# Recurrent outer-product attention and an MLP on one core: odd heads without a second load of v, and 48 weight columns for the state's products

## The chip, the cores and the metric

One core of one Trainium2 chip runs the whole program. The metric is the device time of one execution in microseconds (us). Three runs of the kernel before gave 453.13, 453.8 and 453.02 us, median 453.13. Engine names as in the profile: PE is TensorE (PEld its weight loads), DVE is VectorE, ACT is ScalarE, POOL is GpSimd, SP is SyncE, which here only issues DMAs.

## What is computed

```python
# q, k, v, f_logit: (B=4, H=8, S=768, D=48), float32
f = 1.0 / (1.0 + np.exp(-f_logit))
for t in range(S):
    state = f[:, :, t, :, None] * state + np.einsum('bhd,bhe->bhde', k[:, :, t], v[:, :, t])
    y[:, :, t] = np.einsum('bhd,bhde->bhe', q[:, :, t], state)
x = y.transpose(0, 2, 1, 3).reshape(B, S, 384)
xn = (x - mean(x)) / np.sqrt(var(x) + 1e-06) * g_ln
out = x + np.maximum(xn @ w_ch1, 0.0) @ w_ch2        # 384 -> 1536 -> 384
```

Each head carries a 48 x 48 state that decays by a gate per row; the heads' outputs of one time step are joined to a row of 384, and a two-layer MLP with a residual follows.

## The kernel before

**Tiling.** The sequence is cut into 12 units of 64 time steps; a unit has all 4 batches and 8 heads. In a tile of raw input, 128 partitions are two batches of 64 steps (index `b`, 0 or 1, is the half), and `g` (0 or 1) counts the two such pairs of batches. Heads go in pairs: `a` (0 to 3) is the pair, `r` (0 or 1) the head in it, and `e` (0 to 7) runs over `g` and `a`. Transposed tiles have the pair's two heads on partitions 0 to 47 and 64 to 111 (`head_rows(r)`), and 16 segments `2e + b` of 64 steps along the free axis. `half(i)` is partitions 64i to 64i+63.

**Attention of a unit n**, as a table of stages that `attention(n)` returns:
- `gates`, `after`, `upto` (L686, L701, L705): sigmoid of the transposed gate logits on ACT (L691 from unit 5 on), then two scans on DVE (L664, L676) that give products of gates from each step to the unit's end and from its start.
- `k`, `q` (L709, L722): keys times `after` give kh (L718), queries times `upto` give qh (L727).
- `kept` (L731): state times the unit's whole product, on DVE.
- `carried` (L739, matmul L748): qh times `kept` into the PSUM tile py, 32 matmuls of 48 x 64 weights and 48 columns.
- `scores` (L753, matmul L762): kh times qh into the PSUM tile ps, 32 matmuls; `causal` (L765): DVE masks them into sc.
- `values` (L785, matmul L791): sc times v is added to py, 32 matmuls; then ACT copies py to x (L798), one copy for each g.
- `chunk` (L813, matmul L821): kt times v into the PSUM tile pn, 32 matmuls with 64 weight columns, of which 48 are a head's; `state` (L825): DVE adds pn to `kept` (L829).
- `stats`, `norm`, `turn`: mean and variance on DVE, reciprocal root on POOL, the normalized rows, and their transpose on PE with the gain put on by ACT (L856).

kt is kh transposed. From unit 5 on (`DIRECT`) transposes of f, q, k and kh are not made on PE but by DMA: ACT splits a tile into two planes of 16 bits (`split`, L439), POOL sends them to DRAM (L443: fhalves, khalves, qhalves, Khalves), and SP brings them back with a DMA transpose (`transposed`, L458: `turned` for f and for q in one and the same tile, a tile for k, and kt). The transpose of f can only be issued when DVE has read the same tile as q (L727).

**Where odd heads' v comes from.** Matmul positions are (row half, column half). In `scores`, head r of batch half b puts its 64 x 64 result on PSUM rows `half(b ^ r)`, so for odd heads the two batches are exchanged. `values` therefore needs odd heads' v with the batches exchanged as well, and `load(n, "x")` (L469) fetches them a second time into the tile vx: 4 DMAs a unit, 64 partitions of four runs of 192 bytes each, 48 KB. All of v comes with `load(n, "v")` (L479), 4 DMAs of 96 KB.

**MLP of a unit** (`mlp(n)`): the first layer is L968 in units 0 to 2 and block products (`by_blocks`, L906, with ACT copies L911 and DVE additions L914) from unit 3 on; the second layer is L978 in units 0 and 1 and seven half-size products (L997) after. The output is written by SP (L985, L1010). Weights come as 64-bit floats in 12 pieces through DMAs of 768 KB (L540), and are made 32-bit by ACT, DVE and POOL (L552 to L568) in the first 80 us.

**Order.** Nothing is scheduled by a program: `START` (units 0 to 2 of the MLP) and `UNIT` (one unit of the MLP from 3 on) are plans written by hand, and every engine and every DMA queue takes its instructions in the order in which the tokens stand there. `a5.chunk` is a stage, `m4` a step of the MLP, `l6v` a load, `p6k0` a split, `x6f` a DMA transpose. In `UNIT`, `l{p}x` stands ahead of `p{p}k0`, `l{p}q` and the transpose of f, `x{p}f`.

**PSUM.** Eight banks: four single ones for the MLP and the transposes, two for py, and two with the tag "two" that ps and pn use in turn.

Of the kernel before, what the change touches and what calls it, by code (L numbers as in the profile page):

```python
# [8 lines left out]
FP32 = mybir.dt.float32  # L9
# [294 lines left out]


START = """
l0k a0.gates l0q f d d a0.after l0x d r l0v a0.kx
a0.upto f a0.kept l1f a0.k l1k d a0.q f a0.carried a0.scores a0.causal
a0.values l1q w d r d a0.stats l1x f a0.kt a1.gates w
a0.norm d a1.after l1v a0.chunk a0.turn f r a0.state a1.upto m0 d  # L310
a1.kept w a1.kx f a1.k m0 a1.q f r a1.kt r w
a1.carried d a1.scores a1.causal f l2k f l2v f w m0 a1.values
l2f r r a1.stats a1.chunk w m0 a1.norm m0 a1.turn r m0
m1 r w m1 r w l2x w f l2q w m1
f m1 a1.state a2.gates a2.after r m1 a2.kx m0 m0 r w
a2.k l3k w a2.upto a2.kept m1 a2.q m0 m0 m0 a2.carried l3q
m0 a2.scores l3v l3x a2.causal U m1 a2.values a2.stats l3f a2.norm m1
m1 m1 a3.gates m1 a2.kt m1 a2.turn a2.chunk a3.kx m2 l4f a3.after
U a3.k a3.upto U T m2 a2.state m2 a3.q a3.kept m2 a3.carried
a3.scores a3.kt U U l4v l4k a4.gates a3.causal U U U t  # L320
U a3.values a3.chunk l4q T l5v a4.after m2 l5f U a3.stats m2
a4.kx U l5k a3.norm s2 m2 p5f0 a3.state m2 a4.k U m2
p5f1 m2 a4.kt a3.turn u l6f x5f p5k0 a4.upto a4.q l4x p5k1
y3 l5q a5.gates l5x m2 m2 a4.kept m2
"""
UNIT = """
m{m} a{o}.after a{n}.kt m{m} a{n}.carried p{o}q0 a{n}.scores m{m} p{o}q1 a{n}.causal m{m} m{m}
l{p}k m{m} m{m} a{o}.upto a{n}.values x{o}q x{o}k m{m} a{n}.stats p{p}f0 p{p}f1 m{m}
m{m} a{n}.chunk m{m} a{n}.norm m{m} m{m} m{m} m{m} s{m} m{m} l{p}x p{p}k0
p{p}k1 l{p}q m{m} a{o}.q m{m} x{p}f a{n}.turn a{o}.k l{p}v p{o}K0 a{p}.gates m{m}  # L330
a{n}.state l{z}f a{o}.kept m{m} y{n} m{m} m{m} p{o}K1
"""
# [3 lines left out]
def kernel(  # L336
# [19 lines left out]
    nc = tc.nc  # L356
    B, H, S, D = q.shape
    P = 128
    T = 64
    G = B // 2  # L360
    NP = H // 2
    GA = G * NP
# [25 lines left out]
    raws = fast.enter_context(tc.tile_pool(name="raws", bufs=2))  # L388
# [8 lines left out]
    def two_banks(name, tag="two"):  # L397
        return ps2.tile([P, 2, 512], FP32, tag=tag, name=name)
# [8 lines left out]
    for name, fill in (("f", 40.0), ("q", 0.0), ("k", 0.0)):  # L407
        t = consts.tile([P, G, H, 64], FP32, name=f"{name}raw")
        nc.gpsimd.memset(t[:, :, :, D:64], fill)
        wide_heads[name] = t  # L410
    loaded = {}
# [8 lines left out]
    def raw_of(n, name):  # L420

        return wide_heads["k" if n >= DIRECT and name == "q" else name]
# [38 lines left out]
    def load(n, name, engines=(nc.sync,)):  # L461
        if n >= NU:
            return
        if name == "x":

            loaded[n, name] = raws.tile([P, G, NP, D], FP32, tag="rawx", name=f"vx{n}")
            odd = v.rearrange("b (a r) s d -> b r s a d", r=2)
            for b in range(B):
                nc.sync.dma_start(out=loaded[n, name][(1 - b % 2) * T:(2 - b % 2) * T, b // 2],  # L469
                                  in_=odd[b, 1, n * T:(n + 1) * T])  # L470
            return
        if name == "v":
            vt = raws.tile([P, G, H, D], FP32, tag="rawv", name=f"v{n}")
            loaded[n, name] = vt
        else:
            loaded[n, name] = raw_of(n, name)
        src = {"f": f_logit, "k": k, "q": q, "v": v}[name]
        for b in range(B):
            engines[b % len(engines)].dma_start(  # L479
                out=loaded[n, name][(b % 2) * T:(b % 2 + 1) * T, b // 2, :, 0:D],  # L480
                in_=src[b, :, n * T:(n + 1) * T, :].rearrange("h p d -> p h d"))

    load(0, "f", (nc.sync, nc.scalar))

    power = consts.tile([P, 2], FP32)
# [22 lines left out]
    least = consts.tile([P, NS], FP32)  # L508
    nc.vector.memset(least, 1.0)
    state = consts.tile([P, 2, GA, D], FP32)  # L510

# [122 lines left out]
    def half(i):  # L634
        return slice(64 * i, 64 * i + 64)

    def head_rows(par):
        return slice(64 * par, 64 * par + D)

    def attention(n):  # L640
# [5 lines left out]
        at = {}  # L646
# [92 lines left out]
        def do_carried():  # L739

            at["py"] = py = two_banks(f"py{n}", "out")
            if not n:
                return
            qh, kept = at["qh"], at["kept"]
            for e in range(GA):
                for b in range(2):
                    for r in range(2):
                        nc.tensor.matmul(py[half(b), r, e * D:(e + 1) * D],  # L748
                                         lhsT=qh[head_rows(r), 2 * e + b],
                                         rhs=kept[head_rows(r), b, e], start=e == 0, stop=False,  # L750
                                         skip_group_check=True)

        def do_scores():  # L753


            at["ps"] = ps = two_banks(f"ps{n}").rearrange("s r (e t) -> s r e t", t=T)
            kh, qh = at["kh"], at["qh"]
            for e in range(GA):
                for b in range(2):
                    for r in range(2):  # L760
                        seg = 2 * e + b
                        nc.tensor.matmul(ps[half(b ^ r), r, e], lhsT=kh[head_rows(r), seg],  # L762
                                         rhs=qh[head_rows(r), seg], start=True, stop=True)

        def do_causal():  # L765
# [17 lines left out]
                nc.scalar.copy(out=kt[:, g * NP:(g + 1) * NP], in_=pt)  # L783

        def do_values():  # L785
            py, sc, vt, vx = at["py"], at["sc"], loaded[n, "v"], loaded[n, "x"]
            for e, (g, a) in enumerate(pairs):
                for b in range(2):
                    for r in range(2):
                        rows = half(b ^ r)  # L790
                        nc.tensor.matmul(py[half(b), r, e * D:(e + 1) * D], lhsT=sc[rows, r, e],  # L791
                                         rhs=vx[rows, g, a] if r else vt[rows, g, 2 * a],
                                         start=n == 0 and e == 0, stop=True,
                                         skip_group_check=True)
            x_of[n] = x = xs.tile([P, G, DM], FP32, tag="x", name=f"x{n}")
            pyv = py[:, :, 0:GA * D].rearrange("t r (g a d) -> t g r a d", g=G, d=D)
            for g in range(G):
                nc.scalar.copy(out=x[:, g].rearrange("t (a r d) -> t r a d", r=2, d=D),  # L798
                               in_=pyv[:, g])

        def do_stats():
            x = x_of[n]
# [10 lines left out]
        def do_chunk():  # L813

            if n < NU - 1:
                at["pn"] = pn = two_banks(f"pn{n}")
                kt, vt = at["kt"], loaded[n, "v"]
                for e, (g, a) in enumerate(pairs):
                    for r in range(2):
                        for b in range(2):  # L820
                            nc.tensor.matmul(pn[half(r), b, e * D:(e + 1) * D],  # L821
                                             lhsT=kt[half(b), e, half(r)],
                                             rhs=vt[half(b), g, 2 * a + r], start=True, stop=True)

        def do_state():  # L825
            if n < NU - 1:
# [5 lines left out]

        return {"gates": do_gates, "after": do_after, "upto": do_upto, "kx": do_k_across,
                "k": do_k, "q": do_q, "kept": do_kept, "carried": do_carried,
                "scores": do_scores, "causal": do_causal, "kt": do_kt, "values": do_values,
                "stats": do_stats, "chunk": do_chunk, "state": do_state,
                "norm": lambda: normalize(n), "turn": lambda: turn(n)}

# [290 lines left out]
```

## Time and profile before

| | |
|---|---|
| runs | 453.13, 453.8, 453.02 us |
| profiled execution: span | 453.4 us (the page gives no time for it beside the span) |
| PE busy | 430.9 us, 95% of the span |
| PEld busy | 398.2 us, 88% |
| DVE busy | 330.3 us, 73% |
| ACT busy | 194.4 us, 43% |
| POOL busy | 145.6 us, 32% |
| mean granted TensorE clock | 0.985 |
| packets of SP's DMA queue | 182368, 49.70 MB, 58.5% of 16 engines' span |
| x copies, L798 on ACT | 24, 128x384, 475 ns each |
| issues of vx, L469 on SP | 48, median 614 ns each, 2.5 us from issue to landing |

The span runs from the first to the last instruction of one profiled execution. A line of a view names the source line, the engine, the operation, the tiles (written <- read) and a shape; of a matmul the shape is weights rows*columns and then the moving data. One float32 matmul leaves two records on PE, so 32 matmuls are "x64". "idle before" is what the engine waited, with what released it. The letters after SP and POOL in "SPq" mean the engine's queue, where DMAs are issued one after another.

### The profile page before, as it was taken

The numbers are of one execution on the slowest core, as the hardware profiler recorded it, in microseconds if no ns is written. First come the engines' busy times: TensorE is split into PE (matmuls) and PEld (weight loads), VectorE is DVE, ScalarE is ACT, GpSimd is POOL, SyncE is SP. The second block draws the span as 40 slices with busy tenths as digits, with TensorE's granted clock in tenths as the row PEclk, the third lists the DMA queues.
The fourth block names the chain that finished last, engine by engine and source line by source line (L and its number), as shares of the span: only waits on it lengthen the run. The fifth ranks groups of instructions, "written<-read, shape, count | busy, mean of one in ns | idle before, by whom it ended". The sixth has DMA issues, their size and how long they took to land.

```text
span 453.4 us, 12917 instructions
## 1 busy us (share of the span) xinstructions
PE 430.9 (95%) x5427; PEld 398.2 (88%) x5427; DVE 330.3 (73%) x528; ACT 194.4 (43%) x333; POOL 145.6 (32%) x165
## 2 busy tenths in 40 slices
PE   5689999999999999989999999999999999999993
PEld 4568886667899999989999989989999999999993
DVE  6698867553778988867888878878878778665451
ACT  2275753003234546445556356445455443241320
POOL 2213543249714124223323323324224204011020
PEclk9799999999999999989999999999999999999998
DMA  8999988251736779895889999898997781500001
GB/s 140 193 179 255 234 183 163 49 107 41 130 69 136 187 132 214 197 215 132 208 157 208 181 225 176 198 164 196 204 180 195 177 145 44 97 2 19 19 9 34
DMA packets 188690, 65.68 MB, mean 145 GB/s; under 512 B 175568, under 2 KB 181200, under 8 KB 188624
## 3 DMA queue, kind: packets, MB, share of 16 engines
q1 hardware_dynamic: 182368, 49.70, 58.5%
q0 software_dynamic: 4480, 14.68, 9.2%
q8 instruction: 44, 0.72, 0.7%
q10 hardware_dynamic: 1776, 0.40, 0.5%
q14 instruction: 22, 0.18, 0.2%
HBM read 30.67 MB, written 19.40 MB: 110 GB/s over the span
## 4 chain that ended last, share of the span: by engine, by line
PE 69%; DMA 11%; issue 6%; SPq 5%; POOL 4%; DVE 3%; ACT 1%; POOLq 0%; DVEq 0%; ACTq 0%
PE pp L997 24%; PE ph L968 9%; PE bx L906 8%; PE po L978 6%; PE by L906 6%; DMA kt<-Khalves 5%; SPq L479 3%; DMA w_0words<-in_moe_w_ch_dram 3%; PE pn L821 2%; PE py L748 2%; PE tr L656 2%; PE bz L906 2%; PE ps L762 2%; SPq L1010 2%; PE xp L854 2%
## 5 line engine op out<-in xcount | busy, mean ns | idle before, releaser
L917 ACT ACTIVATE h<-h 128x512 f32<-128x512 f32 x45 | 28.1, 630 | 54.4 <-DVE h L914 50.4
L968 PE MATMUL ph<-xt,w 128*128 128x256 f32 x216 | 48.6, 381 | 0.6 <-ACT xt L856 0.6
L968 PEld LDWEIGHTS ph<-xt,w 128*128 128x128 f32 x216 | 40.3, 190 | 6.3 <-issue 0.8
L997 PE MATMUL pp<-mixed,h 128*128 128x192 f32 x240 | 42.4, 326 | 0.0
L997 PE MATMUL pp<-mixed,s 128*128 128x192 f32 x240 | 42.0, 326 | 0.0
L997 PE MATMUL pp<-w,h 128*128 128x192 f32 x240 | 40.7, 326 | 0.0
L997 PEld LDWEIGHTS pp<-mixed,h 128*128 128x128 f32 x240 | 39.5, 190 | 0.3 <-ACT xt L856 0.3
L997 PEld LDWEIGHTS pp<-mixed,s 128*128 128x128 f32 x240 | 39.1, 190 | 0.0
L997 PEld LDWEIGHTS pp<-w,h 128*128 128x128 f32 x240 | 38.8, 190 | 0.0
L914 DVE TENSOR_TENSOR h<-h,bx 128x512 f32<-128x512 f32 x27 | 18.6, 687 | 24.8 <-PE bx L906 24.8
L1005 POOL TENSOR_TENSOR p1x<-p,x 128x192 f32<-128x192 f32 x10 | 13.1, 1311 | 71.6 <-ACT p L1012 71.6
L978 PE MATMUL po<-w,h 128*128 128x384 f32 x96 | 32.7, 490 | 0.7 <-POOL w L568 0.7
L664 DVE TENSOR_TENSOR_SCAN after<-gates,ends 128x1040 f32<-128x1040 f32 (+1 forms) x13 | 29.6, 2278 | 5.0 <-ACT gates L696 3.0
L676 DVE TENSOR_TENSOR_SCAN upto<-gates,starts 128x1040 f32<-128x1040 f32 (+1 forms) x13 | 30.1, 2314 | 0.5
L856 ACT ACTIVATE xt<-xp,gain 128x128 f32<-128x128 f32 x72 | 20.0, 376 | 23.3 <-PE xp L854 23.3
L906 PE MATMUL bx<-y,v 128*128 128x128 f32 x216 | 29.4, 279 | 0.0
L914 DVE TENSOR_TENSOR h<-h,by 128x512 f32<-128x512 f32 x36 | 24.6, 682 | 5.2 <-PE by L906 5.0
L978 PEld LDWEIGHTS po<-w,h 128*128 128x128 f32 x96 | 17.6, 190 | 12.1 <-POOL w L568 1.3
L809 POOL TENSOR_SCALAR rstd<-mv 128x2 f32<-128x2 f32 x12 | 2.8, 235 | 78.1 <-DVE mv L808 78.1
L906 PEld LDWEIGHTS bx<-y,v 128*128 128x128 f32 x216 | 26.2, 192 | 0.5
L568 POOL TENSOR_TENSOR w<-w_0upper,w_0units 128x768 int32<-128x768 int32 x7 | 12.7, 1814 | 32.8 <-DVE w_0upper L566 27.6
L997 PE MATMUL pp<-w,s 128*128 128x192 f32 x120 | 21.1, 326 | 0.0
(163 smaller groups left out, 971.7 us busy)
## 6 DMA issues: line engine op xcount, KB each, us to landing
w_0words<-in_moe_w_ch_dram SPq DMA_DIRECT2D x7, 768.0 KB, 7.2
kraw<-in_k_dram SPq DMA_DIRECT2D x48, 96.0 KB, 3.6
v<-in_v_dram SPq DMA_DIRECT2D x48, 96.0 KB, 3.8
fraw<-in_f_logit_dram SPq DMA_DIRECT2D x46, 96.0 KB, 3.6
fhalves<-fplanes POOLq DMA_DIRECT2D x14, 256.0 KB, 4.8
khalves<-kplanes POOLq DMA_DIRECT2D x14, 256.0 KB, 3.8
qhalves<-qplanes POOLq DMA_DIRECT2D x14, 256.0 KB, 3.4
Khalves<-Kplanes POOLq DMA_DIRECT2D x14, 256.0 KB, 3.7
```

What stands on the lines that cost most here:

```text
L479: engines[b % len(engines)].dma_start(out=loaded[n, name][(b % 2) * T:(b % 2 + 1) * T, b // 2, :, 0:D], in_=src[b, :, n * T:(n + 1) * T, : ...
L568: nc.gpsimd.tensor_tensor(out=to.bitcast(I32), in0=upper, in1=units, op=ALU.add)
L664: nc.vector.tensor_tensor_scan(out=at["after"].rearrange(flat)[:, c0:c1][:, ::-1], data0=gt[:, c0 + 1:c1 + 1][:, ::-1], data1=ends.rearran ...
L676: nc.vector.tensor_tensor_scan(out=at["upto"].rearrange(flat)[:, c0:c1], data0=gt[:, c0:c1], data1=starts.rearrange(flat)[:, c0:c1], initi ...
L856: nc.scalar.mul(out=xt[:, m, g * P:(g + 1) * P], in_=pt[:, m], mul=gain[:, m:m + 1])
L906: nc.tensor.matmul(banks[bank][:, i], lhsT=right[:, i * P:(i + 1) * P], rhs=left, start=new and i == 0, stop=True, skip_group_check=True)
L914: nc.vector.tensor_tensor(out=out[to], in0=out[to], in1=bank, op=op)
L917: nc.scalar.activation(out=out[to], in_=out[to] if bank is None else bank, func=AF.Relu)
L968: nc.tensor.matmul(ph[:, j], lhsT=w1[:, m, (i + j) * P:(i + j + 1) * P], rhs=xt[:, m], start=m == 0, stop=m == KD - 1)
L978: nc.tensor.matmul(po, lhsT=h[:, i, g * P:(g + 1) * P], rhs=w2[:, i], start=i == 0, stop=i == KF - 1)
L997: nc.tensor.matmul(pp, lhsT=a[:, i], rhs=b[:, i], start=i == 0, stop=i == KH - 1)
L1005: engine.tensor_tensor(out=to, in0=x1, in1=x2, op=op)
```

## The change

Three things, and what follows from them:

1. `load(n, "x")` and all its tokens are gone: 48 DMAs on SP's queue. Both heads of a pair read v from the one tile vt.
2. `scores` now leaves head r on PSUM rows `half(b)`; `values` takes its weights and v from partitions `half(b)`, and writes to `half(b ^ r)`; so does `carried`. So in py the odd heads have the batches exchanged, and the copy to x puts them right: one ACT copy of 128 partitions for the even heads, and two of 64 partitions for the odd heads, which read one half and write the other.
3. `chunk` loads 48 weight columns (`head_rows(r)`), not 64 (`half(r)`), and writes 48 PSUM rows. As `state` still reads all 128 rows, ps and pn are now one tile `shared`, allocated once, so that the 16 rows not written have numbers from the scores in them. They are used by no product.

```diff
-        if name == "x":
-            loaded[n, name] = raws.tile([P, G, NP, D], FP32, tag="rawx", name=f"vx{n}")
-            odd = v.rearrange("b (a r) s d -> b r s a d", r=2)
-            for b in range(B):
-                nc.sync.dma_start(out=loaded[n, name][(1 - b % 2) * T:(2 - b % 2) * T, b // 2],
-                                  in_=odd[b, 1, n * T:(n + 1) * T])
-            return
...
+    shared = two_banks("shared")
...
-                        nc.tensor.matmul(py[half(b), r, e * D:(e + 1) * D],
+                        nc.tensor.matmul(py[half(b ^ r), r, e * D:(e + 1) * D],
...
-            at["ps"] = ps = two_banks(f"ps{n}").rearrange("s r (e t) -> s r e t", t=T)
+            at["ps"] = ps = shared.rearrange("s r (e t) -> s r e t", t=T)
...
-                        nc.tensor.matmul(ps[half(b ^ r), r, e], lhsT=kh[head_rows(r), seg],
+                        nc.tensor.matmul(ps[half(b), r, e], lhsT=kh[head_rows(r), seg],
...
-                        rows = half(b ^ r)
-                        nc.tensor.matmul(py[half(b), r, e * D:(e + 1) * D], lhsT=sc[rows, r, e],
-                                         rhs=vx[rows, g, a] if r else vt[rows, g, 2 * a],
+                        nc.tensor.matmul(py[half(b ^ r), r, e * D:(e + 1) * D],
+                                         lhsT=sc[half(b), r, e], rhs=vt[half(b), g, 2 * a + r],
...
-            for g in range(G):
-                nc.scalar.copy(out=x[:, g].rearrange("t (a r d) -> t r a d", r=2, d=D),
-                               in_=pyv[:, g])
+            nc.scalar.copy(out=xv[:, 0], in_=pyv[:, 0])
+            for b in range(2):
+                nc.scalar.copy(out=xv[half(b), 1], in_=pyv[half(1 - b), 1])
...
-                at["pn"] = pn = two_banks(f"pn{n}")
+                at["pn"] = pn = shared
...
-                            nc.tensor.matmul(pn[half(r), b, e * D:(e + 1) * D],
-                                             lhsT=kt[half(b), e, half(r)],
+                            nc.tensor.matmul(pn[head_rows(r), b, e * D:(e + 1) * D],
+                                             lhsT=kt[half(b), e, head_rows(r)],
```

In the plans only the tokens `l0x` to `l5x` and `l{p}x` are taken out; the order of the rest stays.

More of the change, by code (lines that the diff above doesn't have):

```diff
@@ L306 @@
 START = """
-l0k a0.gates l0q f d d a0.after l0x d r l0v a0.kx
+l0k a0.gates l0q f d d a0.after d r l0v a0.kx
 a0.upto f a0.kept l1f a0.k l1k d a0.q f a0.carried a0.scores a0.causal
-a0.values l1q w d r d a0.stats l1x f a0.kt a1.gates w
+a0.values l1q w d r d a0.stats f a0.kt a1.gates w
 a0.norm d a1.after l1v a0.chunk a0.turn f r a0.state a1.upto m0 d
@@ L313 @@
 l2f r r a1.stats a1.chunk w m0 a1.norm m0 a1.turn r m0
-m1 r w m1 r w l2x w f l2q w m1
+m1 r w m1 r w w f l2q w m1
 f m1 a1.state a2.gates a2.after r m1 a2.kx m0 m0 r w
 a2.k l3k w a2.upto a2.kept m1 a2.q m0 m0 m0 a2.carried l3q
-m0 a2.scores l3v l3x a2.causal U m1 a2.values a2.stats l3f a2.norm m1
+m0 a2.scores l3v a2.causal U m1 a2.values a2.stats l3f a2.norm m1
 m1 m1 a3.gates m1 a2.kt m1 a2.turn a2.chunk a3.kx m2 l4f a3.after
@@ L322 @@
 a4.kx U l5k a3.norm s2 m2 p5f0 a3.state m2 a4.k U m2
-p5f1 m2 a4.kt a3.turn u l6f x5f p5k0 a4.upto a4.q l4x p5k1
-y3 l5q a5.gates l5x m2 m2 a4.kept m2
+p5f1 m2 a4.kt a3.turn u l6f x5f p5k0 a4.upto a4.q p5k1
+y3 l5q a5.gates m2 m2 a4.kept m2
 """
@@ L328 @@
 l{p}k m{m} m{m} a{o}.upto a{n}.values x{o}q x{o}k m{m} a{n}.stats p{p}f0 p{p}f1 m{m}
-m{m} a{n}.chunk m{m} a{n}.norm m{m} m{m} m{m} m{m} s{m} m{m} l{p}x p{p}k0
+m{m} a{n}.chunk m{m} a{n}.norm m{m} m{m} m{m} m{m} s{m} m{m} p{p}k0
 p{p}k1 l{p}q m{m} a{o}.q m{m} x{p}f a{n}.turn a{o}.k l{p}v p{o}K0 a{p}.gates m{m}
@@ L785, in do_values @@
         def do_values():
-            py, sc, vt, vx = at["py"], at["sc"], loaded[n, "v"], loaded[n, "x"]
+            py, sc, vt = at["py"], at["sc"], loaded[n, "v"]
             for e, (g, a) in enumerate(pairs):
@@ L795, in do_values @@
             x_of[n] = x = xs.tile([P, G, DM], FP32, tag="x", name=f"x{n}")
-            pyv = py[:, :, 0:GA * D].rearrange("t r (g a d) -> t g r a d", g=G, d=D)
-            for g in range(G):
-                nc.scalar.copy(out=x[:, g].rearrange("t (a r d) -> t r a d", r=2, d=D),
-                               in_=pyv[:, g])
+            xv = x.rearrange("t g (a r d) -> t r g a d", r=2, d=D)
+            pyv = py[:, :, 0:GA * D].rearrange("t r (g a d) -> t r g a d", g=G, d=D)
+            nc.scalar.copy(out=xv[:, 0], in_=pyv[:, 0])
+            for b in range(2):
+                nc.scalar.copy(out=xv[half(b), 1], in_=pyv[half(1 - b), 1])
         def do_stats():
```

## Prediction

> **What bounds the kernel now.** PE is busy for 430.9 of 453.4 us, so I read the busy time by stretches first, cut where a unit's first block product (bw) starts.
>
> ```profile
> core 0: us, PE busy (x) PEld busy (x) DVE busy (x) ACT busy (x) POOL busy (x), PEclk, DMA share, GB/s
> 185.00:221.10 36.10, 34.39 (x468) 33.64 (x467) 27.15 (x47) 19.75 (x31) 11.09 (x14) 0.95 0.87 185
> 221.10:253.80 32.70, 32.70 (x468) 31.99 (x468) 27.14 (x47) 15.89 (x27) 11.08 (x14) 1.00 0.86 184
> 253.80:287.50 33.70, 32.85 (x468) 32.06 (x468) 26.87 (x47) 18.12 (x30) 11.08 (x14) 1.00 1.00 198
> 287.50:321.10 33.60, 32.77 (x468) 32.02 (x468) 26.97 (x47) 17.34 (x29) 11.09 (x14) 1.00 0.89 187
> 321.10:354.50 33.40, 32.78 (x468) 32.03 (x468) 26.98 (x47) 17.78 (x29) 11.08 (x14) 1.00 0.91 194
> ```
>
> The second of these units is solid PE work, 32.7 us. Four others have the same work and take 36.1, 33.7, 33.6 and 33.4: 3.4 + 1.0 + 0.9 + 0.7 = 6.0 us over. Second, the PE timeline, to see where.
>
> ```profile
> 196.72 1.06 PE L906 MATMUL bz<-xt,v 128*128 128x128 f32 x8
> 199.49 1.15 PE L821 MATMUL pn<-v,kt 64*64 64x48 f32 x64 [1.71 <-DMA kt<-Khalves]
> 200.57 1.85 PE L906 MATMUL bx<-y,w 128*128 128x128 f32 x8
> 202.22 1.91 PE L906 MATMUL by<-y,w 128*128 128x128 f32 x8
> ...
> 234.90 1.16 PE L906 MATMUL bx<-y,w 128*128 128x128 f32 x8
> ```
>
> Each time it is `chunk` waiting for the DMA transpose that makes kt: 1.71 us here, then 0.75, 0.8 and 0.6. After the longest one the products run at half clock (1.85 us for what takes 1.16), which is the rest of the 3.4 us. Third, the queue that issues this transpose:
>
> ```profile
> 261.57 2.48 SPq L458 DMA_TRANSPOSE kt<-Khalves  x1
> ...
> 274.26 2.58 SPq L469 DMA_DIRECT2D vx<-in_v_dram  x4
> 276.94 2.67 SPq L479 DMA_DIRECT2D kraw<-in_q_dram  x4
> 279.71 1.25 SPq L1010 DMA_DIRECT2D out_dram<-p1x  x2
> 281.12 3.05 SPq L458 DMA_TRANSPOSE turned<-fhalves  x1
> ...
> 294.56 2.58 SPq L458 DMA_TRANSPOSE kt<-Khalves  x1
> ```
>
> From one kt to the next SP is never free for more than 0.3 us: 33.0 us of issuing, or of waiting inside an issue, in a unit whose PE work is 32.7. SP's queue, with 0.87 to 1.00 of the DMA engines' time beside it, sets the pace by a hair, and PE catches the difference at kt.
>
> **What the Trainium skill says.** (1) "TensorE: Matmul & The Clock Gate", section "LDWEIGHTS (loading the stationary operand)": a load takes its columns / 1.2 ns, whatever its rows, 0.83 ns a column. The trace agrees in slope: the loads of 1, 64 and 128 columns last 84, 135 and 190 ns, 0.8 to 0.9 ns a column. (2) Same page, "The mechanism": a load overlaps matmuls in flight only where the row group differs. The trace has orders that alternate the row half at every matmul (`carried`, `scores`) and one that doesn't (`values`), at one speed (below). (3) Same page, "What's actually happening": after an idle window of about 3.4 us the clock is halved. The trace's clock records show 0.5 from 200.9 to 204.3 us, though PE idled only 1.7 us of the window; waits of 0.6 to 0.8 did not do it. (4) "DMA: Bandwidth & Descriptors", "Issuing engines are not separate DMA queues": spreading DMAs over engines saves only the issue time, which is usually small. Here it is not small: SP's issue time fills the unit.
>
> **The change part by part.**
>
> *The loads of vx.* Removed: 4 issues a unit, 2.58 us and four gaps of 0.04, so 2.7 us of SP's 33.0; and DMA work: the packet records have 18.3 ns for a mean packet of 192 bytes, 1024 packets over 16 engines, 1.17 us a unit. In the four late units the wait of kt is cut as follows. kt is issued behind the last output and behind Khalves, whose second part ACT makes only after the gates, and these wait for the transpose of f. That transpose can go out earlier by SP's gain, but not before DVE has finished qh on the same tile: qh ends at 177.7, 246.5, 280.2 and 313.8 in these units, and the transpose was issued at 178.7, 249.0, 281.1 and 316.1. So f, and with it gates, Khalves and kt, move ahead by 0.9, 2.4, 0.9 and 2.2 us at least, and by up to 1.17 more where the queue ahead of it is drained sooner. The waits are 1.71, 0.75, 0.8, 0.6. The last three go. Of the first up to 0.8 may stay, or nothing; I take 0.4 and, as waits under 0.8 left the clock whole, the half-clocked 1.7 us go too. Sum: 6.0 - 0.5 = 5.5 us, bounds 2.5 (half of it, if Khalves' own way through DRAM holds kt back) and 6.0. Late next is nothing in sight: the unit at 221 shows all five engines keep 32.7 us.
>
> *The same loads in the start.* PE has idle time there that hangs on data: the chain goes through the first weight pieces (landing 15.2, 22.3 us), gates of unit 1 and the first MLP products at 28.9, and a last piece at 79.5 us (a wait of 0.72 <- POOL w). In front of the second piece stand the four vx of unit 0, in front of the last one twelve. DMA engines are at 0.87 and 1.02 of their time in 0 to 20 and 20 to 40 us, so I count DMA time and not issues: 1.17 us less ahead of the second piece, 3.5 us less ahead of the last. From 29 to 180 us PE is solid but for the 0.72. So 1.17 + 0.72 = 1.9 at best; ACT's copies and DVE's order in between may keep some: I take 1.4, bounds 0 and 2.6 (if the 2.6 us of issue, not DMA time, were what counts). The v load itself, which is now first, released `values` of unit 0 with a wait of only 0.2 us.
>
> *48 weight columns.* In `chunk` and its three sister groups PE starts four matmul passes in a bunch, and a bunch every 58.5 ns:
>
> ```profile
> 230.72 0.22 PE L791 MATMUL py<-v,sc 64*64 64x48 f32 x1
> 230.72 0.22 PE L791 MATMUL py<-vx,sc 64*64 64x48 f32 x1
> 230.73 0.22 PE L791 MATMUL py<-v,sc 64*64 64x48 f32 x1
> 230.74 0.22 PE L791 MATMUL py<-vx,sc 64*64 64x48 f32 x1
> 230.78 0.22 PE L791 MATMUL py<-v,sc 64*64 64x48 f32 x1
> ```
>
> The start records give 58.5 ns in all four groups: with 64 moving columns (`scores`) and with 48 (the others), with 48 rows and with 64. What they have in common is 64 weight columns, and 64 x 0.83 = 53 ns, plus 5. With 128 weight columns, N=192 and N=256 passes take 162 and 217 ns, so 0.83 ns a moving column as well, with 2 to 4 ns on top. So a bunch costs the longer of load and moving, plus about 5. `chunk` after has 48 and 48: 40 + 5 = 45 ns. 16 bunches x 13.5 = 0.22 us, x 11 units (the twelfth has no chunk) = 2.4 us, all on PE's own path; I take 2.3. The other bound is 0: if it is the moving side that doesn't go under 64 columns, or the bunch of four, nothing changes. It can't cost more: neither the number of matmuls nor their halves of the array change in it. I give 2.3 two chances in three.
>
> *Positions in `carried`, `scores`, `values`.* `carried` and `scores` exchange orders, each measured at 58.5 ns. `values` went (row, column) 00, 10, 11, 01 and goes 00, 01, 11, 10, that is the same ring backwards, with the same PSUM bank for each position. Cost nil; bounds in the second rival.
>
> *Copies to x.* Three for two on ACT, 384 columns each at 475 ns; two started and ended within 0.84 us, so +0.42 us a unit, 5 us of ACT. Behind it on ACT stand the copy h<-bx, two plane copies of f and the copy h<-bz; behind that PE's second use of these banks. In the unit at 221 the x copies end at 232.07, and DVE comes to the statistics only at 233.31, after the scan; h<-bx ends at 232.7 and PE writes that bank again at 234.9; h<-bz ends at 235.1, PE needs it at 236.8. Every slack exceeds 0.42. In the unit at 254 ACT is later (bz ends at 268.7, its bank is due at 270.5, and 0.8 earlier with the stall gone): 1.0 left. Cost nil; if the cover were gone, 0.42 x 12 = 5 us at most.
>
> *One tile for ps and pn.* They had the same two banks in turn before, with the same readers between; no new wait for PE.
>
> *Sum.* 5.5 + 1.4 + 2.3 = 9.2 us off a span of 453.4, so 444.2; the median of the runs is 0.3 under the span, so 443.9 us, which I round to 444.
>
> **Rivals.**
> - *The columns don't count* (chunk stays at 58.5 ns a bunch): 453.1 - 6.9 = 446.2. For: moving data was never under 48 there, and no group has fewer weight columns.
> - *`values` slows, slower than before.* A row half given twice running, first of all at the start of each bunch (00, 01), lets the second load not overlap, and each bunch then needs two loads in turn: 53 ns more x 16 x 12 units = 10.2 us on PE, so 453.1 - 9.2 + 10.2 = 454.1. It decides from 0.77 us a unit on. Against: the ring before also has two pairs of one row half in four.
> - *The wait is moved, not removed.* kt is still late because Khalves goes through ACT, POOL and DRAM in any case (Khalves landed at 261.5, kt was issued at 261.6). Half of the 6.0 comes back, and the start gives nothing: 453.1 - 3.0 - 2.3 = 447.8, or 450.1 without the columns.
> - *The load wasn't late for anyone*: the waits return at another transpose on SP, as DMAs now start earlier and collide. Then only the columns, or nothing: 450.8 to 453.
>
> **How the numbers follow.** All as forecast (442 to 446): 0.52. Columns don't count (445 to 448): 0.20. Wait moved in part (447 to 450.5): 0.13. Nothing gained, within 0.2% (0.9 us, about what a measurement of this kernel can tell from no change): 0.06. Slower, by `values` or by a copy that isn't covered: 0.09. The range takes in the first three: 442.0 at the lower end (6.0 + 2.4 + 2.6 = 11.0 off) to 450.5. Faster 0.85, same 0.06, slower 0.09.
>
> **What would show it.** In the profile after: no wait of PE at pn, or one under 0.5 us; units of about 32.5 us; no half clock near 200 us; chunk bunches 45 ns apart, loads of pn near 122 ns; SP with 2 to 3 us free a unit; the second weight piece landing 1 us earlier. I am wrong if pn still waits for kt, if the bunches of `values` are over 60 ns apart, or if DVE's statistics wait for ACT in every unit.

## The result and the profile after

| | before | after |
|---|---|---|
| median of 20 runs each, same chip | 452.31 us (448.89 to 461.23) | 448.06 us (446.23 to 454.66) |
| ratio | | 0.9925, 95% interval 0.9902 to 0.9947 |
| profiled execution: span | 453.4 us | 444.6 us (its own time 446.23) |
| mean granted TensorE clock | 0.985 | 0.992 |

The change makes the kernel faster by 0.75%, or by 4.3 us between the medians; 9.1 us were forecast. Single executions of either kernel scatter by several us; the ratios leave out disturbed runs (over 1.5% above a kernel's fastest), which also cuts off executions with long waits at kt, so the median of all runs is given beside each ratio. Both profiled executions are far from typical. That of after was the fastest of its 20. Its time is its span + 1.6 us; the kernel before, profiled again below, shows span + 1.7, which puts the first profiled execution of before at about 455.1: 2.0 us above the median of the three runs that the prediction had and 2.8 above the 452.31 here, and not within 0.3 us of it. So the two spans, 8.8 us apart, flatter the change.

The same stretches as in the prediction, in the kernel after (the units from the first block product at 181.6 on):

```profile
core 0: us, PE busy (x) PEld busy (x) DVE busy (x) ACT busy (x) POOL busy (x), PEclk, DMA share, GB/s
181.60:214.90 33.30, 32.50 (x468) 31.72 (x467) 26.95 (x46) 19.98 (x32) 11.10 (x14) 1.00 0.88 191
214.90:247.40 32.50, 32.50 (x468) 31.79 (x467) 27.01 (x46) 18.14 (x30) 11.10 (x14) 1.00 0.87 192
247.40:279.90 32.50, 32.50 (x468) 31.79 (x467) 27.02 (x46) 17.59 (x30) 11.09 (x14) 1.00 0.88 188
279.90:312.40 32.50, 32.50 (x468) 31.80 (x467) 27.01 (x46) 19.03 (x32) 11.09 (x14) 1.00 0.92 193
312.40:345.20 32.80, 32.55 (x468) 31.78 (x467) 27.05 (x46) 18.64 (x31) 11.10 (x14) 1.00 0.82 191
```

Three of five units are solid PE work, 32.5 us where before a solid one had 32.7. The first and the last are longer; the PE timeline shows the first of these two:

```profile
193.37 1.06 PE L899 MATMUL bz<-xt,v 128*128 128x128 f32 x8
195.22 0.94 PE L814 MATMUL shared<-v,kt 64*48 64x48 f32 x64 [0.80 <-DMA kt<-Khalves]
```

`chunk` takes 0.94 us instead of 1.15, and a wait of 0.80 us for kt is still ahead of it. SP's queue from one unit to the next, in the kernel after:

```profile
197.42 4.76 SPq L458 DMA_TRANSPOSE qraw<-khalves  x1
204.16 2.68 SPq L471 DMA_DIRECT2D kraw<-in_q_dram  x4
206.89 1.32 SPq L1003 DMA_DIRECT2D out_dram<-p1x  x2
208.37 2.26 SPq L458 DMA_TRANSPOSE turned<-fhalves  x1
210.73 2.74 SPq L471 DMA_DIRECT2D v<-in_v_dram  x4
213.51 2.67 SPq L471 DMA_DIRECT2D fraw<-in_f_logit_dram  x4
216.29 1.94 SPq L1003 DMA_DIRECT2D out_dram<-u4y  x2
218.32 1.19 SPq L1003 DMA_DIRECT2D out_dram<-u4x  x2
219.61 2.15 SPq L1003 DMA_DIRECT2D out_dram<-u2x  x2
221.87 1.79 SPq L458 DMA_TRANSPOSE kt<-Khalves  x1
```

SP is now free, but in one place only: between 202.18 and 204.16, ahead of the load of q's rows into kraw. What it waits for there is in the waits of SP's queue from 150 to 380 us (total, times, longest), first in the kernel before, then after:

```profile
SPq L479 <- ACT kplanes L439: 3.5, 3, 2.6
```

```profile
SPq L471 <- ACT kplanes L439: 21.2, 7, 5.1
```

q's rows go into the tile that k's rows leave, and its first half comes free only when ACT has made the first of the two copies that split k (`kplanes`, 203.08 to 205.08 here for both). From that load to kt SP's queue is as full as it was: 17.7 us, and 17.6 before (276.94 to 294.56 in the lines of the prediction). That is where the freed 2.7 us of a unit went: 21.2 - 3.5 = 17.7 us over seven units, 2.5 us each, are now a wait for ACT at the one point ahead of the run that ends in kt.

Last, the weight loads of `chunk` (min/median/max ns), before and after:

```profile
L821 PEld LDWEIGHTS pn<-v,kt x704: 129/135/135, 25.2 to 368.1; 64*64 64x64 f32 x176
```

```profile
L814 PEld LDWEIGHTS shared<-v,kt x704: 116/122/122, 22.7 to 358.6; 64*48 64x48 f32 x176
```

### The profile page after: what moved, and what is told of

It reads as the page before. It is cut to its first block, busy times and chain, and to the rows that moved or that the text cites. A ratio compares the mean times of both kernels' runs of the same rounds, so it can differ in the third digit from the quotient of the medians.

```text
span 444.6 us, 12872 instructions
## 1 busy us (share of the span) xinstructions
PE 425.5 (96%) x5427; PEld 393.6 (89%) x5427; DVE 332.4 (75%) x528; ACT 202.2 (45%) x345; POOL 146.3 (33%) x165
## 4 chain that ended last, share of the span: by engine, by line
PE 82%; DVE 4%; DMA 3%; SPq 3%; issue 2%; POOL 2%; ACT 1%; POOLq 0%; ACTq 0%
PE pp L990 27%; PE ph L961 11%; PE bx L899 10%; PE by L899 7%; PE po L971 7%; PE bz L899 3%; PE tr L649 3%; DMA kt<-Khalves 2%; PE shared L755 2%; PE py L783 2%; PE py L741 2%; PE shared L814 2%; SPq L1003 2%; PE xp L847 2%; PE bv L899 2%
## 5 line engine op out<-in xcount | busy, mean ns | idle before, releaser
L971 PEld LDWEIGHTS po<-w,h 128*128 128x128 f32 x96 | 17.7, 190 | 11.0
L963 ACT ACTIVATE h<-ph 128x512 f32<-128x512 f32 x18 | 10.7, 594 | 28.9 <-PE ph L961 28.7
```

The costliest lines, as they stand in the source:

```text
L971: nc.tensor.matmul(po, lhsT=h[:, i, g * P:(g + 1) * P], rhs=w2[:, i], start=i == 0, stop=i == KF - 1)
```

## The experiments

Each ratio is to the kernel before on the same chip; "all" is the median of all runs. Where two kernels are compared, the difference of the ratios is taken of 452 us, and its interval is about 2 us to both sides. The time outside the span is not the same in every kernel: at the median 1.7 us before and 1.5 after, but 2.4 in edge_dve and 2.6 in dead_start.

### Both kernels again

No edit. `before_again`: 

> The kernel before once more, unchanged, to see how far single executions of it differ. Theory A (the profiled execution of before was a slow one: its waits at pn and its half clock are not in every execution): median of the runs 450 to 452.5 us, and this profile has other waits of PE at pn than the 3.9 us of the first, and a half clock in the middle or none. Theory B (each execution has the same waits, the clock of the chip differs): the waits at pn come again within 0.5 us, at the same units.

`after_again`: 

> The changed kernel once more, unchanged. Theory A: median 447 to 448.5 us; the profile of a typical execution has a span 1 to 2 us over the 444.6 of the first, as waits of PE at pn or in the start that the first had not (it was the fastest of 20). Theory B: units of 32.5 us without a wait again, and the difference lies outside the span.

`after_third`: 

> The changed kernel, unchanged, on the chip of the next three. From its two earlier measurements (ratios 0.9925 and 0.9901 to the kernel before, bounds 0.987 to 0.9947): 0.987 to 0.995, some 447.5 us at a kernel before of 451.5. In its trace PE waits about 1 us at xp near 49 us and 0.6 to 0.9 us at pn near 195 us, and the last attention unit is 31.8 us long.

`after_fourth`: 

> The changed kernel, unchanged, on the chip of the next three. Three measurements so far: ratios 0.9925, 0.9901, 0.9921 to the kernel before. 0.989 to 0.995; first block product at 149 to 151.5 us, waits at pn of 0.8 to 1.8 us in all.

Measured: before_again 0.9977 (0.995 to 1.0004), all 451.24. The kernel after 0.9901 (0.987 to 0.9933), 0.9921 (0.9892 to 0.995) and 0.9917 (0.9885 to 0.9948); all 447.35, 448.58 and 448.86 on three chips. With the first ratio their mean is 0.9916, a gain of 3.8 us. 69 executions of the kernel before on one chip lay between 447.2 and 458.1. In this second profile of the kernel before (span 451.1, its own time 452.82, close to the median) two of the four units that had waited run without a wait:

```profile
core 0: us, PE busy (x) PEld busy (x) DVE busy (x) ACT busy (x) POOL busy (x), PEclk, DMA share, GB/s
186.80:219.50 32.70, 32.70 (x468) 32.00 (x467) 26.89 (x46) 17.98 (x29) 11.07 (x14) 1.00 0.93 201
...
252.20:286.10 33.90, 32.79 (x468) 32.04 (x467) 26.97 (x46) 17.79 (x30) 11.08 (x14) 1.00 1.04 195
286.10:319.70 33.60, 32.74 (x468) 32.00 (x467) 26.96 (x46) 19.64 (x31) 11.06 (x14) 1.00 0.92 198
319.70:352.40 32.70, 32.70 (x468) 31.99 (x467) 27.15 (x46) 17.24 (x29) 11.08 (x14) 1.00 0.90 193
```

So this execution has 1.2 + 0.9 = 2.1 us over, no half clock there, and not the 6.0 us that I took away. The four profiles of the kernel after have 1.2, 1.6, 2.2 and 5.5 us over the clean unit of 32.48. Nor do the runs show less half clock after the change: the mean of the granted clock over all runs, on three chips, is 0.9906 to 0.9911 with the kernel before and 0.9896 to 0.9915 with the kernel after.

### The columns and the loads, one without the other

`cols64`, the changed kernel with the old weight columns, and `only48`, the kernel before with the new ones and the shared tile:

```diff
 cols64 (to after)
-  nc.tensor.matmul(pn[head_rows(r), b, ...], lhsT=kt[half(b), e, head_rows(r)],
+  nc.tensor.matmul(pn[half(r), b, ...], lhsT=kt[half(b), e, half(r)],
 only48 (to before)
+  shared = two_banks("shared")
-  nc.tensor.matmul(pn[half(r), b, ...], lhsT=kt[half(b), e, half(r)],
+  nc.tensor.matmul(pn[head_rows(r), b, ...], lhsT=kt[half(b), e, head_rows(r)],
```

> The changed kernel with 64 weight columns in chunk again (loads of vx stay away). Forecast's step: the 48 columns are worth 0.22 us a unit on PE's own path, 2.4 us in all, so 450 to 451 us and a bunch of four passes of pn at 58.5 ns. Rival: part of the columns' gain is only slack ahead of kt (PE that is faster waits longer), so less, 448.5 to 449.5 us.

> The kernel before with 48 weight columns in chunk and one tile for ps and pn, loads of vx and positions as before. Forecast's step: 2.4 us under before, about 449.5 to 450 us, if PE's path is what counts. Rival: SP's queue, which fills the unit with 33.0 us, keeps its pace, PE waits at pn for what it saves: 451.5 to 452.5 us, as before, with longer waits at pn.

Measured on one chip, with before_again and after_again: cols64 0.9966 (0.9941 to 0.9991), all 450.21; only48 0.9982 (0.9949 to 1.0015), all 452.1. Alone the columns bring 0.8 us that can't be told from nothing, and the rest of the change 1.5. The columns on top of the rest bring 0.9966 - 0.9901 = 0.0065, 2.9 us, or 2.9 between the medians of all runs. Both together bring 4.5 us on this chip, 2.1 more than the two alone. By the ratios that gap is no larger than its interval of 2.4. By the medians of all runs (452.01 before) it is 2.9 us, and drawing the recorded times again at random leaves about 1 to 5: it is likely there, its size is open.

PE saves the same in each kernel: a solid unit is 32.70 us long with 64 columns and 32.48 with 48, in all profiles. My reading is that with the loads still there PE has the shorter unit, but SP has not, so that PE gives the 0.22 us back as a longer wait for kt, and the unit is as long as the slower of the two. The waits of PE in only48 fit (3.9 and 2.0 us in the two profiles before), but this was one of its longest executions, 457.78 us:

```profile
PE shared L822 <- DMA kt<-Khalves: 8.8, 4, 3.9
```

### The loads put back where nobody reads them

All these are the changed kernel with loads at their old places into a tile of their own, which nothing reads:

```diff
 dead_full: all 48 loads
+        if name == "x":
+            spare = raws.tile([P, G, NP, D], FP32, tag="rawx", name=f"vx{n}")
+            for b in range(B):
+                nc.sync.dma_start(out=spare[(1 - b % 2) * T:(2 - b % 2) * T, b // 2],
+                                  in_=odd[b, 1, n * T:(n + 1) * T])
 dead_issue: the same 48 issues, with 16 rows of 192 bytes each
+                nc.sync.dma_start(out=spare[at:at + 16, b // 2, 0:1],
+                                  in_=odd[b, 1, n * T:n * T + 16, 0:1])
 dead_data: a unit's packets in one issue
+            nc.sync.dma_start(out=spare, in_=v[n % B, :, at:at + P].rearrange("h p d -> p h d"))
 dead_start: of dead_full the tokens l0x to l5x alone; dead_units: l{p}x alone
```

> The changed kernel with the 48 loads of vx put back where they stood, into a tile that nobody reads. Theory A (the loads are what matters, positions and copies cost nothing): as with the columns alone, 451 to 453 us. Rival (the three copies or the new positions take back part of the gain): over that, 453.5 us or more, with PE waiting for ACT.

> The changed kernel with the 48 issues put back, but each of 16 rows of 192 bytes, a sixteenth of the data. Theory A1 (SP's issue time fills the unit, 2.7 us of 33): most of the loss is back, 450.5 to 452.5 us. Theory A2 (the 1.17 us a unit of DMA engine time counts, SP only waits inside issues): near the changed kernel, 447 to 448.5 us.

> The changed kernel with the same number of packets of 192 bytes a unit put back, but in one issue and not four. Theory A1: near the changed kernel, 447.5 to 449 us. Theory A2: most of the loss is back, 450.5 to 452.5 us.

> The changed kernel with the 24 loads of units 0 to 5 put back, at their old places, into a tile that nothing reads. If the start is where most of the loads' cost was: 2.5 to 3.5 us more than the changed kernel on this chip, the first block product near 153, and waits at pn as in the changed kernel. If my 1.4 us for the start was right: 1.0 to 1.8 more, the first block product 1.4 later.

> The changed kernel with the 24 loads of units 6 to 11 put back into a tile that nothing reads. If the loads cost little at kt in a usual execution: 0.5 to 2.5 us more than the changed kernel, as waits at pn, with the load of q's rows issued 22.5 to 24 us after a unit's first block product and not at 21.83. If my 5.5 us was right: 4.5 to 6 more.

Measured: dead_issue 0.9918 (0.9879 to 0.9956), dead_data 0.9915 (0.9883 to 0.9947): neither costs anything that can be told from the changed kernel's 0.9916. dead_full 0.9936 (0.99 to 0.9972), but all 456.04, against 454.68 for the kernel before on that chip; its runs go up to 461.5. By that median it has the rival's number, but not the rival's sign: PE waits 6.1 us for kt, and for ACT no longer than in the kernel after. dead_start 0.9929 (0.9905 to 0.9954), 0.5 us more than after_fourth on its chip, under both of my two ranges. dead_units 1.0006 (0.9978 to 1.0035), 4.0 us more than after_fourth, and 4.3 between the medians of all (453.17 and 448.86): with its loads in the late units alone the changed kernel is back at the time of the kernel before. The waits of PE point the same way, in dead_units first (profiled in one of its longer executions, 455.5 us) and then in dead_start (in one of its shorter ones, 446.8):

```profile
PE shared L821 <- DMA kt<-Khalves: 7.0, 4, 3.5
```

```profile
PE shared L821 <- DMA kt<-Khalves: 0.6, 1, 0.6
```

So neither A1 nor A2 holds: the issues or the data alone cost nothing that shows, and both together 4 us. That fits the hole in SP's queue: it is 2.5 us a unit; the short issues take 2.0 us of SP, the one long issue 0.6, and the full loads 2.6 us and four gaps. What is left of the 21.2 us that SP waits for kplanes is, in dead_data, dead_issue and dead_full:

```profile
SPq L476 <- ACT kplanes L439: 14.0, 7, 4.5
```

```profile
SPq L479 <- ACT kplanes L439: 6.3, 5, 1.9
```

```profile
SPq L478 <- ACT kplanes L439: 1.2, 2, 1.1
```

The hole is used up where time is lost, and not where none is; dead_units, with 5.3 us left in its long execution, lies close to dead_issue. No run widens the hole and leaves the loads in, so this stays a reading. My expectation for dead_units, with 0.5 to 2.5 us on the one side and 4.5 to 6 on the other, was met on neither side.

### The third copy

`two_copies` and `kt_first_two` (the latter on top of kt_first, below) make two copies of 128 partitions, and so leave out the exchange of the odd heads' batches:

```diff
-            nc.scalar.copy(out=xv[:, 0], in_=pyv[:, 0])
-            for b in range(2):
-                nc.scalar.copy(out=xv[half(b), 1], in_=pyv[half(1 - b), 1])
+            for r in range(2):
+                nc.scalar.copy(out=xv[:, r], in_=pyv[:, r])
```

> The changed kernel with two copies of 128 partitions to x, as before; left out is the exchange of odd heads' batches, so x has them at the wrong batch. Forecast's step (the third copy is hidden everywhere): no change, 447 to 447.8 us. Rival (in the start the third copy makes PE wait at xp near 49 us for 1.08 us, and 0.26 us in the last unit): about 1.3 us less, 446 us.

> kt_first with two copies of 128 partitions to x in each unit instead of three; it leaves out the exchange of odd heads' batches. With no waits at pn to blur it, the third copy shows itself alone: 0.85 us less than kt_first by the traces so far (0.6 at xp near 49 us, 0.26 in the last unit), ratio near 0.9865. If the copy costs nothing, as I forecast: 0.9884, within the interval of kt_first; if it costs its 0.42 us in every unit: 5 us less.

Measured: two_copies 0.9849 (0.981 to 0.9888), all 446.69, 3.0 us under the mean of the kernel after; kt_first_two 0.9875 (0.9843 to 0.9908), 0.4 under kt_first, both differences with intervals of 2 us and more. The traces are sharper. In the six profiles of the kernel after, dead_start and kt_first PE waits 1.08 or 1.09 us at xp near 50 us, in both with two copies 0.49; and the last attention unit, from its first block product to that of the next, takes 31.78 to 31.79 us with three and 31.53 with two. The idle time of PE at xp from 45 to 52 us, with what ended it, in the kernel after and in two_copies:

```profile
  ACT xt L849: 1.1, 1
```

```profile
  DVE xn L836: 0.5, 1
```

So the copy costs 0.6 + 0.25 = 0.85 us by the traces, where no wait or queue covers it: in the start and at the end. By the time alone it is between nothing and 5 us. kt_first_two was to show it with no wait for kt beside it, and does not: PE waits for kt once again, 0.35 us, and two of its full units are 2.2 and 0.8 us longer than the clean one.

### DVE makes the second half copy

`edge_dve`, in units 0, 1 and 11:

```diff
-                nc.scalar.copy(out=xv[half(b), 1], in_=pyv[half(1 - b), 1])
+                copy = nc.vector.tensor_copy if b and n in (0, 1, NU - 1) else nc.scalar.copy
+                copy(out=xv[half(b), 1], in_=pyv[half(1 - b), 1])
```

> In units 0, 1 and the last, DVE and not ACT makes the second of the two half copies to x, so that ACT has two copies as before the change. If the third copy costs time where nothing covers it, at the start and at the end: the wait of PE at xp near 49 us goes from 1.08 to about 0.5, the last attention unit from 31.79 to about 31.5, 0.6 to 0.85 us less in all. If the copy was not what those waits hang on: both stay, and the time within 0.3 us.

Measured: 1.003 (1.0003 to 1.0058), all 452.45: 4.9 us more than after_third on the same chip, 3.9 between the medians of all runs, on the wrong side of both theories. In the two profiles the first block product of a full unit comes 3.8 us later (155.3 and 151.5), so most of the loss lies in the start. The DVE timeline in the start of edge_dve, and then that of after_third:

```profile
19.05 0.55 DVE L793 COPY x<-py 64x384 f32<-64x384 f32 x1 [2.27 <-PE idle L575]
19.62 0.56 DVE L554 TENSOR_SCALAR w_0body<-w_0upper 128x768 f32<-128x768 f32 x1
...
21.68 0.56 DVE L801 BATCH_NORM_STATS2 stats<-x 128x6 f32<-128x384 f32 x1
```

```profile
16.50 0.55 DVE L554 TENSOR_SCALAR w_0body<-w_0upper 128x768 f32<-128x768 f32 x1
...
19.95 0.56 DVE L800 BATCH_NORM_STATS2 stats<-x 128x6 f32<-128x384 f32 x1 [1.31 <-ACT x L792]
```

On DVE the copy stands, by the written order, ahead of three instructions on a weight piece, which until then had filled the time in which `values` ran. Now DVE sits idle for 2.27 us until the copy's data are there, the weight piece follows after it, and the statistics start 1.7 us later. PE's waits at xp for DVE's rows in the start go from 1.5 to 3.9 us. The gain of one short instruction on ACT was bought with three that lost their place on DVE.

### What still holds kt

`own_f` gives the transpose of f a tile of its own and moves its transpose ahead of the stage `q`; `both` is own_f and edge_dve:

```diff
-            turned["f"] = turned["q"] = late["pool"].tile([P, NS, T], FP32, name="turned")
+            turned["q"] = late["pool"].tile([P, NS, T], FP32, tag="turnedq", name="turned")
+            turned["f"] = late["pool"].tile([P, NS, T], FP32, tag="turnedf", name="turnedf")
-p{p}k1 l{p}q m{m} a{o}.q m{m} x{p}f a{n}.turn ...
+p{p}k1 l{p}q x{p}f m{m} a{o}.q m{m} a{n}.turn ...
```

> Only the transpose of f is changed: it gets a tile of its own, so that it need not wait for DVE's qh, and goes out ahead of the scatter for q. Theory A, that what still holds kt after the change is f's transpose behind qh: the waits at pn (0.8 near 195 us, and 0.2 to 0.6 later) go, 1.0 to 1.5 us less than the changed kernel on this chip. Theory B, that SP's order ahead of kt (three outputs issued right before it) or the way of Khalves through DRAM holds it: the waits stay within 0.3 us, and the time within 0.5 us.

> The two edits together. If both theories hold: 1.6 to 2.3 us less than the changed kernel on this chip, about 445.5 at a kernel before of 451.5. If only the copies count 0.6 to 0.85 less; if only f's transpose counts 1.0 to 1.5 less; if neither, within 0.5.

Measured: own_f 0.9987 (0.9951 to 1.0023), all 451.68, 3.0 us more than after_third; both 1.0114 (1.0078 to 1.0149), all 455.5, 8.7 more, about the sum of the two losses. No theory had a loss. It is not f's wait for qh that holds kt. SP's queue in own_f (profiled at 456.1 us, its longest execution; the order and the lengths are what counts here):

```profile
206.44 2.69 SPq L472 DMA_DIRECT2D kraw<-in_q_dram  x4
209.22 3.50 SPq L459 DMA_TRANSPOSE turnedf<-fhalves  x1
...
225.58 1.96 SPq L459 DMA_TRANSPOSE kt<-Khalves  x1
```

f's transpose goes out directly behind q's rows, but stays in SP's queue for 3.50 us, not 2.26; over all its units the median is 3.26, and 1.9 in after_third. From q's rows to kt SP needs 19.1 us, 17.7 in the kernel after. f came sooner, kt later.

`kt_first` leaves all that as in the changed kernel, and moves a unit's last six outputs, u4y, u4x and u2x, behind the next kt. The token o issues what is held; u4x and u2x are held as u4y is, and in the last unit nothing is:

```diff
-        put(u4y, 1, right)
+        held.append(lambda: put(u4y, 1, right))
...
-m{m} a{o}.after a{n}.kt m{m} a{n}.carried ...
+m{m} a{o}.after a{n}.kt o m{m} a{n}.carried ...
```

> The changed kernel with six issues moved: the outputs u4y, u4x and u2x of a unit stand behind the transpose of kt on SP's queue, not ahead of it. Theory A, that SP's queue from the release of q's rows to kt is what still makes kt late: kt goes out about 2 us sooner (bounded by the landing of Khalves), all waits at pn go, and the time is 0.8 to 1.8 us under the changed kernel, near 447. Theory B, that Khalves' own way or the transfer of kt holds it: the waits stay and the time is within 0.5. A third way: the six outputs delay k's next rows and the transposes behind, and waits turn up at another transpose; then slower.

Measured: 0.9884 (0.9837 to 0.9931), all 446.14, where after_fourth on the same chip has 0.9917 and 448.86: 1.5 us less by the ratios, whose intervals overlap, and 2.7 between the medians. Its six runs lie between 445.31 and 447.89, so all under the other's median. The trace is plain: its waits of PE have no entry for kt at all, and every full unit but one is 32.48 us. SP's queue:

```profile
178.87 2.73 SPq L471 DMA_DIRECT2D v<-in_v_dram  x4
181.64 2.97 SPq L471 DMA_DIRECT2D fraw<-in_f_logit_dram  x4
187.08 1.40 SPq L458 DMA_TRANSPOSE kt<-Khalves  x1
188.57 1.52 SPq L1004 DMA_DIRECT2D out_dram<-u4y  x2
190.19 1.25 SPq L1004 DMA_DIRECT2D out_dram<-u4x  x2
191.54 2.50 SPq L1004 DMA_DIRECT2D out_dram<-u2x  x2
```

kt goes out 5.1 us after the unit's first weight load (0.16 us ahead of its first block product), where after_fourth has 7.4. SP stands idle from 184.6 to 187.1 until Khalves has landed, and can: its unit has that much to spare now.

`kt_first_before` makes the same move in the kernel before.

> The kernel before, with its vx loads, its 64 weight columns and its two copies, and the six outputs moved behind kt on SP's queue as in kt_first. If the loads cost time only through kt's place on SP's queue: no waits at pn, units of 32.70 us, the first block product as in the kernel before, and 1.5 to 3 us less than the kernel before (ratio 0.993 to 0.997). If the loads fill SP's unit whatever the order: waits at pn or at another transpose stay, and the ratio is over 0.998.

Measured: 1.0084 (1.0053 to 1.0115), all 454.29, 4.1 us more than the kernel before on its chip. SP's queue and, in a second view, the waits of PE:

```profile
183.41 2.67 SPq L479 DMA_DIRECT2D fraw<-in_f_logit_dram  x4
191.22 1.95 SPq L458 DMA_TRANSPOSE kt<-Khalves  x1
...
206.45 2.65 SPq L469 DMA_DIRECT2D vx<-in_v_dram  x4
209.19 2.65 SPq L479 DMA_DIRECT2D kraw<-in_q_dram  x4
```

```profile
PE pn L821 <- DMA kt<-Khalves: 5.5, 5, 1.9
```

Here SP idles 5.1 us ahead of kt as well, but has no free time to pay for it: everything behind is late by as much, vx and q's rows too (25.4 us after the unit's first weight load, 21.83 when nothing is late), and then the next kt. All its six runs lie over the eleven of the kernel before on that chip. The one edit is worth some -2 us with the loads gone (1.5 to 2.7, see above) and +4 with them there.

## Why the prediction was wrong

The direction, the place and the columns' price per unit were right; the size was twice what was measured (9.1 us forecast, 3.8 by the mean of four ratios). By its steps:

- **The base, "the median is 0.3 under the span".** Time and span are not the same scale: the time is span + 1.5 to 1.7. The profiled execution was some 2 us above the median of the three runs shown. What made it longer was taken off as if every execution had it.
- **"6.0 - 0.5 = 5.5 us" at kt.** This is the step that failed most. The 6.0 were those of one long execution; one closer to the median has 2.1 (before_again). And 1.2 to 2.2 us stay in three of four profiles after, 5.5 in the fourth, not 0.5. (Nor was the lower bound of 2.5 the half of it that it was said to be: half is 3.0 of the 6.0, or 2.75 of the 5.5.) From 2.1 to some 1.7 is half a microsecond on view, and between the means of these few profiles (4.0 and 2.6) it is 1.4; the term was about four times too large or more. What the loads' removal does in the units shows in the time with the columns in place: dead_units, +4.0 us. My reading is that it keeps SP's unit under PE's shorter one, so that the columns' gain isn't given back. But six late units gain only 1.3 us by the columns, so where the rest of the 4.0 us (interval 2) comes from is open. In the profiles of dead_units and only48, both long executions, the longest wait (3.48 and 3.92 us) was followed by half clock, which makes a wait cost more than its length.
- **"f, and with it gates, Khalves and kt, move ahead by 0.9, 2.4, 0.9 and 2.2 us".** I looked for the floor of f's transpose in DVE's qh. The floor lies earlier in SP's queue: q's rows can't be loaded before ACT has split k, 21.83 us after the unit's first weight load in each clean unit of the kernel after. In the kernel before the load was issued at 22.4 to 25.5, and where PE itself was late the split was late with it. So only a part of 2.7 us could move kt; the rest is the 2.5 us a unit of new waiting for kplanes. own_f shows that qh was not the floor, and kt_first that the queue behind q's rows is what sets kt.
- **"I take 1.4" for the start.** Not settled. The first block product of a full unit comes at 152.3 and 154.1 us in the two profiles before and at 149.1 to 151.5 in the four after; of the difference of means, 3.3 us, 1.1 are columns (five units) and 2.2 are left, with the third copy's 0.6 already paid out of them. In the other traces it comes at 150.5 to 153.3 us with all of the start's loads in (only48, dead_full, dead_start, kt_first_before) and at 148.4 to 150.4 with none (edge_dve and both apart), 2.4 us between the means, with both column widths on either side. By the time, dead_start has 0.5 us with an interval of 2. So the term may have been too small; the spread between executions is as large as it.
- **"I take 2.3" for the columns.** Right per unit to the digit: `chunk` starts a bunch every 45 ns, its 64 passes stand 730 ns apart from first to last (930 before), and clean units are 0.22 us shorter. As a term that stands alone it is doubtful: without the loads' removal it brings nothing that can be told (only48), with it 2.9 us.
- **"Cost nil" for the third copy.** I checked the slack in two late units, where it holds. In the start and in the last unit nothing covers it: 0.85 us.
- **Positions in `carried`, `scores`, `values`, and one tile for ps and pn.** Nil, as forecast: 64 passes of `values` still take 930 ns, and no wait of PE for the shared tile's readers appears.

Of the rivals, "the wait is moved, not removed" named the outcome best: 447.8, against 448.06. In part that is luck: it gave the start nothing, and its reason, Khalves' own way through DRAM, is not what kt_first shows: Khalves is early enough, and SP's queue was busy with outputs. The rival `values` slows is out. The sum closes only roughly: 2.4 for the columns (eleven units of 0.22), 2.2 for the start beside them, some 0.5 at kt and -0.25 at the end make 4.9, where 3.8 was measured; the spread of the start alone is larger than the gap.

## What to carry to other kernels

Before a wait is priced from one profile, its execution must be placed among the runs, span and time on one scale, and the kernel profiled a second time: a wait that only one of the two profiles has can't be counted in full. Where two queues run at almost the same pace, don't count on adding up the savings on them; here one alone brought 0.8 us and the other 1.5, and both together 4.5 on the same chip. Time taken out of an in-order queue comes back as idle time at the next thing the queue waits for, so follow it to that point, and then spend it there: the same move of six outputs gained some 2 us where the queue had room and lost 4 where it had none.

## What else the runs showed

- A transpose by DMA that is issued earlier can hold its queue longer: f's, 1.9 us behind the outputs (after_third), 3.26 directly behind a load (own_f).
- The half clock doesn't follow from a wait's length alone: waits at pn of 1.71 us (before) and 2.25 us (after_fourth) brought a window of 3.4 us at 0.5; one of 2.11 us (two_copies) brought none. In the start such windows add up to 3.4 us in two profiles of the kernel after and to 6.8 in the other two, and there is none in dead_units, whose start is the same.
